# Second batch's scores moved ahead of its exps and values, third batch's q loaded first, fourth batch's loads behind a gate

## The chip, the cores and the metric

One core of a Trainium2 chip runs one launch of the kernel. The metric is the device time of one execution in microseconds (us), as the median over runs. The core has TensorE (PE; its weight loads are listed as PEld), VectorE (DVE), ScalarE (ACT), GpSimd (POOL) and SyncE (SP, which here only issues DMAs).

## The reference

Attention with pooled keys and values, then a mixer of two parts. With B = 8 batches, H = 8 heads, S = 576 positions and D = 64:

```
k_p = k.reshape(B, H, S/8, 8, D).mean(axis=3)          # 72 pooled keys; v_p likewise
attn = softmax(q @ k_p.T / sqrt(D)); a = attn @ v_p
x = a as (B, S, 512)
u = x + (relu(x.T @ w_tok1) @ w_tok2).T                # mix over positions, hidden 256
out = u + relu(u @ w_ch1) @ w_ch2                      # mix over channels, hidden 1536
```

All inputs and the output are float32; the kernel works in bfloat16 and casts as it loads.

## The kernel before

Batches are counted from 0. The 576 positions of a batch are 512 "main" rows (four tiles of 128) and 64 "tail" rows. Batches are paired, [0,7], [1,2], [3,4], [5,6], so that two tails share one tile of 128 rows; a pair's first batch has slot 0, the other slot 1. For batches 3 to 6 the tails of a pair's k and q are loaded with its first batch.

*Loads.* All go through GpSimd's DMA queue. `load(b, which)` (L116) issues k (0), q (1) and v (2) in the order given. k and q have two buffers each, v one. From batch 2 on, v comes as 72 rows of 8 positions (L131), and `sum_v` (L292) pools it on GpSimd with 12 additions (L298 to L300). `load_gated` (L737) first copies one column of a tile on GpSimd, so that the loads behind it are issued only when that tile is written, then loads, then pools v. GpSimd does all this in program order: an addition that waits for v holds up the next gate and the next loads.

*Attention.* A `Unit` (L302) holds two of the four main tiles of a batch; a batch has units `a` and `c`, and a `TailUnit` `t`. Their steps: q transposed (qT); scores `do_S` in three banks, each with a maximum and a subtraction on DVE (L329, L331); exps `do_E` on ACT (L339); the probabilities transposed, `do_PT` (pT); values `do_AV` (L387), each half followed by a reciprocal and a product on DVE (L391, L392). For batches 0 and 1 TensorE makes the transposes and DVE or ACT copies them out of PSUM (L352). From batch 2 on, SP issues DMA transposes: `qT_dma` (L538), pT (L346, L445).

*Mix over positions.* `mix_stream` (L567) adds `do_AT` (L472), k pooled for batches that come (`pool_k`: L267 on TensorE, L280 on DVE and ACT), then u (L510) and its transposes uT (L526, by SP's DMA from batch 1 on, one for each of the four tiles).

*Mix over channels.* `c_stream(b)` (L797): GT (L756, 12 tiles of 128 hidden channels), then the output (L771), added to u on DVE (L775) and stored by SP (L803). This is most of TensorE's work.

*Order.* Streams are lists of steps with costs. `weave` (L29) lays the attention and position mix of the next batches between the matmuls of the current batch's channel mix, in proportion to the costs; the order within each engine is then fixed. Beside batch 0's channel mix stand `second_stream` (batch 1's attention and mix, L645) and `score_stream(2)` (L689); beside batch 1's stand `value_stream(2)` (L718) and `score_stream(3)`. `value_stream(2)` begins with `qT_dma(3)` and with `load_gated(4, ...)`, whose gate is batch 2's last pT; its mix pools batch 3's k. `score_stream(3)` pools batch 4's k between its score banks.

Before the manual schedule, the kernel queues batch 1's loads, the last weights, batch 2's loads, batch 3's k and q, and `sum_v(2)`. Batch 3's v follows in `second_stream`, with `sum_v(3)` behind it.

Of the kernel before, what the change touches and what calls it, by code (L numbers as in the profile page):

```python
# [15 lines left out]
class Stream:  # L16
# [5 lines left out]
    def add(self, cost, fn):  # L22
        self.items.append((cost, fn))
# [25 lines left out]
def kernel(  # L49
# [20 lines left out]
    MAIN = NJ * P  # L70
# [37 lines left out]
    x_main, x_tail, u_main, uT_main, u_tail, uT_tail, ATs = {}, {}, {}, {}, {}, {}, {}  # L108
# [7 lines left out]
    def load(b, which=(0, 1, 2)):  # L116
        g = group_of[b]
        if (b == 2 or g > 1 and slot_of[b] == 0) and 0 in which:
            tail_t[b] = [tail_pool.tile([P, H, D], BF16, name=n) for n in ("kt", "qt")]
            if b == 2:  # L120
                for t in tail_t[b]:
                    nc.gpsimd.memset(t[half[0]], 0.0)
            else:
                tail_t[groups[g][1]] = tail_t[b]
        main_t.setdefault(b, [None] * 3)
        for i in which:
            src = (k, q, v)[i]
            if i == 2 and b > 1:

                vs = v_pool.tile([P, H, POOL, D], BF16, name="vs")  # L130
                nc.gpsimd.dma_start(out=vs[0:SP].rearrange("p h t d -> p h (t d)"),  # L131
                                    in_=src[b].rearrange("h (p t) d -> p h (t d)", t=POOL))
                main_t[b][i] = vs
                continue
            mt = (v_pool.tile([P, H, POOL, D], BF16, name="vs")[:, :, 0:NJ, :] if i == 2 else
                  kv_pool.tile([P, H, NJ, D], BF16, name=("km", "qm")[i]))
            main_t[b][i], tt = mt, tail_t[b][i]
            nc.gpsimd.dma_start(out=mt.rearrange("p h j d -> p h (j d)"),
                                in_=src[b, :, 0:MAIN, :].rearrange("h (p j) d -> p h (j d)", j=NJ))

            for bb in [b] if g < 2 else groups[g] if slot_of[b] == 0 else []:
                nc.gpsimd.dma_start(out=tt[half[slot_of[bb]]], in_=src[bb, :, MAIN:S, :].rearrange("h p d -> p h d"))
# [101 lines left out]
    def load_w_ch2():  # L244
        for i in range(3):
            n = NM // 3
            nc.gpsimd.dma_start(out=wc2[:, i * n:(i + 1) * n, :],
                                in_=moe_w_ch2[i * n * P:(i + 1) * n * P, :].rearrange("(c p) n -> p c n", p=P))
# [43 lines left out]
    def sum_v(b):  # L292

        vs, add = main_t[b][2][0:SP], ALU.add
        for h0 in range(0, H, 2):
            hs = slice(h0, h0 + 2)
            s4 = sum_pool.tile([P, 2, 4, D], FP32, name="s4")[0:SP]
            nc.gpsimd.tensor_tensor(out=s4, in0=vs[:, hs, 0:4], in1=vs[:, hs, 4:8], op=add)  # L298
            nc.gpsimd.tensor_tensor(out=s4[:, :, 0:2], in0=s4[:, :, 0:2], in1=s4[:, :, 2:4], op=add)  # L299
            nc.gpsimd.tensor_tensor(out=vpx[b % NB][:, hs, 0:D], in0=s4[:, :, 0], in1=s4[:, :, 1], op=add)  # L300

    class Unit:  # L302
# [40 lines left out]
        def do_PT(self, e):  # L343
            self.pT[e] = pt_pool.tile([P, H, P], BF16, name="pT")
            if not self.by_pe:
                nc.sync.dma_start_transpose(out=self.pT[e], in_=self.probs[:, e].rearrange("p h n -> p (h n)"))  # L346
                return
            pT_ps = ps_tr.tile([SP, H, P], BF16, name="pt")
            for h in range(H):
                nc.tensor.transpose(out=pT_ps[:, h, :], in_=self.probs[:, e, h, 0:SP], identity=ident)  # L350
            by_dve = e == 0 and self.jj == 1 if self.first else e == 1
            (nc.vector.tensor_copy if by_dve else nc.scalar.copy)(out=self.pT[e][0:SP], in_=pT_ps)  # L352

        def do_AV(self, e):
# [189 lines left out]
    KP, VP, QT, SC, PT, AV = 900, 1080, 900, 1060, 700, 1150  # L544
    parts = {}

    def units(b):

        g, s = group_of[b], slot_of[b]
        x_main[b] = x_pool.tile([P, NJ, DM], BF16, name="xm")  # L550
        t = None
        if g < 2:
            t = TailUnit(g, [b])
        elif s == 0:
            x_tail[g] = x_pool.tile([P, DM], BF16, name="xt")
            t = TailUnit(g, groups[g])
        parts[b] = Unit(b, 0), Unit(b, 1), t
        qTs[b] = att_pool.tile([P, 2 * H, P], BF16, name="qT")
        return parts[b]
# [4 lines left out]
    def adder(st):  # L564
        return lambda weight, f, *args, **kw: st.add(weight, lambda: f(*args, **kw))

    def mix_stream(st, b, pooled=()):  # L567

        g, s = group_of[b], slot_of[b]
        add = adder(st)  # L570
        u_main[b] = u_pool.tile([P, NJ, DM], BF16, name="um")
        uT_main[b] = u_pool.tile([P, 4, MAIN], BF16, name="uTm")
        if s == 1:
            u_tail[g] = ut_pool.tile([P, DM], BF16, name="ut")
            uT_tail[g] = ut_pool.tile([P, 4, P], BF16, name="uTt")
        do_AT, do_both_AT, do_u, do_uT = token_mix(b)
        if b == 0:
            return do_both_AT, do_u, do_uT
        add(1080, do_AT, 0)
        add(1080, do_AT, 1)  # L580
        for bb in pooled:
            add(KP, pool_k, bb)
        nj = NJ + s
        for j in range(nj + 1):
            if j < nj:
                add(690, do_u, j)
            if j >= 1:
                add(0 if b else 224, do_uT, j - 1)
# [56 lines left out]
    def second_stream(st):  # L645

        add = adder(st)
        b = 1
        a, c, t = units(b)
        add(QT, a.do_qT)  # L650
        add(QT, c.do_qT)
        add(SC, a.do_S, 0)
        add(VP, pool_v, b)
        add(SC, a.do_S, 1)
        add(0, a.do_E, 0)
        add(SC, a.do_S, 2)
        add(0, a.do_E, 1)
        add(SC, c.do_S, 0)
        add(0, a.do_E, 2)
        add(QT, t.do_qT)  # L660
        add(SC, c.do_S, 1)
        add(0, c.do_E, 0)
        add(PT, a.do_PT, 0)
        add(PT, a.do_PT, 1)
        add(SC, t.do_S)
        add(0, c.do_E, 1)
        add(AV, a.do_AV, 0)
        add(SC, c.do_S, 2)
        add(0, t.do_E)
        add(0, load, 3, (2,))  # L670
        add(0, sum_v, 3)
        add(AV, a.do_AV, 1)
        add(0, c.do_E, 2)
        add(PT, t.do_PT)
        add(PT, c.do_PT, 0)
        add(AV, t.do_AV)
        add(PT, c.do_PT, 1)
        units(2)
        add(0, qT_dma, 2)
        add(AV, c.do_AV, 0)  # L680
        add(AV, c.do_AV, 1)
        mix_stream(st, b, owned(2))

    def owned(b):

        g, s = group_of[b], slot_of[b]
        return [b] if g < 2 else groups[g] if s == 0 else []
# [134 lines left out]
    clear_probs()  # L822
    load(1)
    load_w_ch2()
    load(2)
    load(3, (0, 1))
    sum_v(2)
    engines = {mybir.EngineType.PE, mybir.EngineType.Activation, mybir.EngineType.DVE,
               mybir.EngineType.SP, mybir.EngineType.Pool}
    with tc.manual_schedule(engines=engines):  # L830
        weave(Stream(), first_stream())
        for b in range(B):
            side = Stream()
            if b == 0:
                second_stream(side)
            elif b + 1 < B:
                value_stream(side, b + 1)
            if b + 2 < B:
                score_stream(side, b + 2)

            weave(c_stream(b), side, 3456.0 if b <= 1 else 1728.0, 3456.0 if b == B - 2 else 1728.0)
# [30 lines left out]
```

## Time and profile before

| | us |
|---|---|
| median of 3 runs | 289.02 |
| lowest and highest | 288.86, 290.66 |
| the profiled execution | 290.2 |
| its span | 288.5 |
| TensorE busy in the span | 271.0 (94%) |
| VectorE busy | 162.4 (56%) |
| ScalarE busy | 121.3 (42%) |
| GpSimd busy | 101.5 (35%) |

The span runs from the first to the last instruction of one profiled execution; 1.7 us lie around it. A line of the profile names an engine, a line of the kernel, an operation, the tile that it writes and those that it reads (`out<-in`), and how many such instructions stand together. "<-" in brackets names what ended the idle time before. The granted clock is the share of TensorE's full clock. GpSimd's and SP's DMAs are two queues that share 16 DMA engines.

### The profile page before, as it was taken

Reading aid. Unit: us, or ns where it says so; the run is one execution under the profiler, and the core shown is the slowest. Engines: PE = TensorE matmul, PEld = TensorE weight load, DVE = VectorE, ACT = ScalarE, POOL = GpSimd, SP = SyncE. Lnnn points to the kernel's source line nnn. Section 1 sums busy time; section 2 is a strip of 40 time slices with the busy share of each in tenths; the row PEclk is TensorE's granted clock in tenths of the full one; section 3 lists DMA queues with packets and bytes.
Section 4 is the critical chain, followed back from the end, with each engine's and each line's share of the span. In section 5 each row is a group of like instructions: output and inputs, shape, how many; then the busy total and the mean of one; then the engine's idle time right before and its main releaser. Section 6 shows DMA issues by size and latency. Waiting matters only on the chain.

```text
span 288.5 us, 5632 instructions
## 1 busy us (share of the span) xinstructions
PE 271.0 (94%) x2210; PEld 147.1 (51%) x2246; DVE 162.4 (56%) x371; ACT 121.3 (42%) x222; POOL 101.5 (35%) x147
## 2 busy tenths in 40 slices
PE   6888998885999999999999999999999999999995
PEld 4554755442445554446545554465445444464463
DVE  4676268687356985386647953684558642530012
ACT  8572887113442355114553365035442561026320
POOL 8666634292780836129508423570000000000000
PEclk9999999999899999999999999999999999999999
DMA  7999999999959999998999799959524820241013
GB/s 84 185 205 198 196 204 192 174 203 146 252 88 169 166 214 195 182 183 166 172 185 155 170 218 153 157 165 162 115 54 97 194 58 36 93 109 39 27 45 110
DMA packets 102714, 42.68 MB, mean 148 GB/s; under 512 B 72480, under 2 KB 98080, under 8 KB 102688
## 3 DMA queue, kind: packets, MB, share of 16 engines
q0 software_dynamic: 36688, 17.93, 47.2%
q1 hardware_dynamic: 65856, 24.26, 43.7%
q8 instruction: 17, 0.28, 0.4%
q10 hardware_dynamic: 144, 0.13, 0.1%
q14 instruction: 9, 0.07, 0.1%
HBM read 35.85 MB, written 9.44 MB: 157 GB/s over the span
## 4 chain that ended last, share of the span: by engine, by line
PE 82%; DMA 7%; DVE 6%; ACT 3%; issue 1%; DVEq 0%
PE pa L756 31%; PE pa L771 28%; DMA qT<-qm 4%; PE pa L510 4%; PE pa L472 4%; PE pa L387 3%; DMA uTm<-um 3%; PE pa L253 2%; PE pa L326 2%; DVE sh L331 2%; DVE mx L329 1%; PE pa L267 1%; ACT prob_m L339 1%; PE pa L518 1%; ACT pT L352 1%
## 5 line engine op out<-in xcount | busy, mean ns | idle before, releaser
L771 PE MATMUL pa<-wc,GT 128*128 128x512 bf16 (+1 forms) x429 | 102.7, 373 | 1.0 <-DVE sh L331 0.2
L756 PE MATMUL pa<-uTm,wc 128*128 128x512 bf16 x357 | 90.1, 384 | 3.8 <-DMA uTm<-um 3.1
L758 ACT ACTIVATE GT<-pa 128x512 bf16<-128x512 f32 x105 | 62.5, 597 | 66.5 <-PE pa L756 62.4
L756 PEld LDWEIGHTS <-wc 128*128 128x128 bf16 x564 | 45.4, 98 | 40.6 <-DVE o L775 3.6
L771 PEld LDWEIGHTS <-GT 128*128 128x128 bf16 x444 | 41.5, 98 | 40.4
L339 ACT ACTIVATE prob_m<-sh 128x432 bf16<-128x432 f32 (+1 forms) x48 | 24.7, 522 | 60.9 <-DVE sh L331 51.1
L298 POOL TENSOR_TENSOR s<-vs 72x512 f32<-72x512 bf16 x24 | 27.6, 1148 | 49.7 <-DMA vs<-in_v_dram 48.2
L775 DVE TENSOR_TENSOR o<-pa,um 128x512 f32<-128x512 f32 (+1 forms) x33 | 22.1, 670 | 25.3 <-PE pa L771 25.3
L329 DVE TENSOR_REDUCE mx<-pa 128x6 f32<-128x432 f32 (+1 forms) x48 | 26.4, 550 | 7.6 <-PE pa L326 7.5
L331 DVE TENSOR_TENSOR sh<-pa,mx 128x432 f32<-128x432 f32 (+1 forms) x48 | 26.8, 558 | 5.1 <-DVE mx L329 0.5
L391 DVE RECIPROCAL den<-pa 128x4 f32<-128x4 f32 (+1 forms) x66 | 11.6, 176 | 24.5 <-PE pa L387 24.4
L515 DVE TENSOR_TENSOR um<-pa,xm 128x512 bf16<-128x512 f32 x30 | 20.2, 687 | 8.6 <-PE pa L510 8.6
L392 DVE TENSOR_TENSOR xm<-pa,den 128x256 bf16<-128x256 f32 x56 | 23.8, 424 | 1.9
L510 PE MATMUL pa<-AT,w2m 128*128 128x512 bf16 x64 | 18.3, 379 | 0.5 <-ACT AT L466 0.5
L299 POOL TENSOR_TENSOR s<-s 72x256 f32<-72x256 f32 x24 | 17.3, 722 | 1.9
L468 DVE TENSOR_SCALAR AT<-pa 128x512 bf16<-128x512 f32 x8 | 5.5, 692 | 21.8 <-PE pa L476 21.1
L387 PEld LDWEIGHTS <-pT 72*128 72x128 bf16 (+1 forms) x280 | 12.4, 100 | 8.8 <-issue 1.7
L326 PE MATMUL pa<-kbd,qT 128*128 128x144 bf16 x128 | 15.5, 226 | 1.4 <-DMA qT<-qm 0.9
L326 PEld LDWEIGHTS <-qT 128*128 128x128 bf16 x128 | 10.7, 98 | 10.5 <-DMA qT<-qm 1.4
L387 PE MATMUL pa<-vpx,pT 72*128 72x65 bf16 (+1 forms) x280 | 14.1, 194 | 1.1 <-DVE pT L352 0.5
L472 PE MATMUL pa<-xm,w1m 128*128 128x512 bf16 x54 | 14.4, 379 | 0.4 <-DVE xm L392 0.2
L253 PE MATMUL pa<-idle 128*128 128x288 bf16 (+2 forms) x40 | 9.8, 379 | 2.3 <-DVE pool_t L178 2.2
(122 smaller groups left out, 232.8 us busy)
## 6 DMA issues: line engine op xcount, KB each, us to landing
out_dram<-o SPq DMA_DIRECT2D x31, 256.0 KB, 2.6
km<-in_k_dram POOLq DMA_DIRECT2D x8, 512.0 KB, 7.7
qm<-in_q_dram POOLq DMA_DIRECT2D x7, 512.0 KB, 12.7
vs<-in_v_dram POOLq DMA_DIRECT2D x6, 576.0 KB, 10.1
wc<-in_moe_w_ch_dram POOLq DMA_DIRECT2D x6, 512.0 KB, 12.4
out_dram<-o SPq DMA_DIRECT2D x9, 128.0 KB, 2.4
vs<-in_v_dram POOLq DMA_DIRECT2D x2, 512.0 KB, 9.9
kt<-in_k_dram POOLq DMA_DIRECT2D x8, 64.0 KB, 7.7
```

What stands on the lines that cost most here:

```text
L298: nc.gpsimd.tensor_tensor(out=s4, in0=vs[:, hs, 0:4], in1=vs[:, hs, 4:8], op=add)
L326: nc.tensor.matmul(out=sc[:, (h - h0) * 2:(h - h0) * 2 + 2, :], lhsT=qTs[self.b][:, 2 * h + self.jj, :], rhs=kbd[self.b % NB][:, h], start ...
L329: nc.vector.tensor_reduce(out=mx[:, 0:n], in_=sc, axis=AX.X, op=ALU.max)
L331: nc.vector.tensor_tensor(out=sh[:, 0:n], in0=sc, in1=mx[:, 0:n, None].broadcast_to([P, n, SP]), op=ALU.subtract)
L339: nc.scalar.activation(out=self.probs[:, :, h0:h1, 0:SP].rearrange("p e h n -> p h e n"), in_=self.sh[i][:, 0:(h1 - h0) * 2].rearrange("p ...
L387: nc.tensor.matmul(out=ao[r, hh, :], lhsT=probs_of(h, r), rhs=vpx[b % NB][:, h, :], start=True, stop=True)
L392: nc.vector.tensor_tensor(out=xo[rows, hf * HP * D:(hf + 1) * HP * D].rearrange("p (h d) -> p h d", d=D), in0=ao[rows, :, 0:D], in1=den[ro ...
L472: nc.tensor.matmul(out=at_ps, lhsT=w1m[:, j, m * P:(m + 1) * P], rhs=x_main[b][:, j, :], start=(j == 0), stop=False)
L510: nc.tensor.matmul(out=u_ps, lhsT=w2m[:, m, j, :], rhs=ATs[b][:, m, :], start=(m == 0 and not by_act), stop=(m == 1))
L756: nc.tensor.matmul(out=g_ps[:, i, :], lhsT=wc1[:, kk, m * P:(m + 1) * P], rhs=uTs[:, kk, :], start=(kk == 0), stop=(kk == 3))
L758: nc.scalar.activation(out=GT[:, m0:m0 + per, :], in_=g_ps, func=AF.Relu)
L771: nc.tensor.matmul(out=hold["ps"], lhsT=GT[:, kk, j * P:(j + 1) * P], rhs=wc2[:, kk, cols], start=(kk == 0), stop=(kk == NM - 1))
```

## The change

In `second_stream`, batch 2's v and `sum_v(2)` are queued behind batch 1's pooled v. The transposes and value products of unit `a` move back behind the tail's scores and the third score bank of unit `c`. `a`'s second value product stands behind the tail's transpose, and both transposes of `c` stand together ahead of the tail's value product. c's second pT copy goes from DVE to ACT. Ahead of the schedule, batch 2's loads are q, then k; batch 3's k and q are no longer queued there. All of batch 3's loads, v too, and `sum_v(3)` stand at the end of `second_stream` behind a gate on the last main tile of batch 1's transposed u.

```
-            by_dve = e == 0 and self.jj == 1 if self.first else e == 1
+            by_dve = e == 0 and self.jj == 1 if self.first else e == 1 and self.jj == 0
...
         add(VP, pool_v, b)
+        add(0, load, 2, (2,))
+        add(0, sum_v, 2)
         add(SC, a.do_S, 1)
...
         add(PT, a.do_PT, 0)
-        add(PT, a.do_PT, 1)
         add(SC, t.do_S)
         add(0, c.do_E, 1)
-        add(AV, a.do_AV, 0)
+        add(PT, a.do_PT, 1)
         add(SC, c.do_S, 2)
         add(0, t.do_E)
-        add(0, load, 3, (2,))
-        add(0, sum_v, 3)
-        add(AV, a.do_AV, 1)
+        add(AV, a.do_AV, 0)
         add(0, c.do_E, 2)
         add(PT, t.do_PT)
+        add(AV, a.do_AV, 1)
         add(PT, c.do_PT, 0)
+        add(PT, c.do_PT, 1)
         add(AV, t.do_AV)
-        add(PT, c.do_PT, 1)
         units(2)
         add(0, qT_dma, 2)
         add(AV, c.do_AV, 0)
         add(AV, c.do_AV, 1)
         mix_stream(st, b, owned(2))
+        add(0, load_gated, 3, lambda: uT_main[b][:, 3, MAIN - 1:MAIN])
...
-    load(2)
-    load(3, (0, 1))
-    sum_v(2)
+    load(2, (1, 0))
```

In the built program the order of TensorE's, DVE's and ACT's instructions differs only inside this stretch, and SP's not at all. GpSimd now works through: batch 2's q, k and v, `sum_v(2)`, the gate, batch 3's seven loads, `sum_v(3)`, the gate of batch 4, batch 4's loads.

## The prediction

> Batches are counted from 0, as in the code: the "second batch" is batch 1, the "third" batch 2, the "fourth" batch 3. Times without a unit are us from the start of the span.
>
> **What bounds the kernel now.** I read the page first (busy shares and the row of the granted clock), then the stretches of 5 us, the chain of waits from 40 to 100, and the timelines of GpSimd and TensorE. TensorE is busy 94% of the span, so only its gaps can be won, and a new gap costs its full length.
>
> ```profile
> PE 271.0 (94%) x2210; PEld 147.1 (51%) x2246; DVE 162.4 (56%) x371; ACT 121.3 (42%) x222; POOL 101.5 (35%) x147
> ```
> The stretches show where the gaps lie: behind "PE" stands its busy time, and the third value from the end is the granted clock.
> ```profile
> 65.00:70.00 5.00, 3.30 (x21) 1.58 (x19) 4.53 (x10) 2.11 (x5) 1.39 (x3) 1.00 1.49 144
> 70.00:75.00 5.00, 3.51 (x9) 1.30 (x10) 1.01 (x2) 1.13 (x3) 1.78 (x2) 0.66 1.15 213
> 75.00:80.00 5.00, 4.95 (x44) 2.58 (x43) 2.88 (x11) 2.98 (x5) 4.53 (x7) 1.00 1.14 251
> ```
> The chain names the causes: the transpose of batch 2's q (qT) is issued at 49.10 and takes 12.50, and the last transpose of batch 1's u (uTm) takes 7.32 from 64.03 to 71.35. Then 16 matmuls take 5.24.
> ```profile
> 49.10 12.50 DMA qT<-qm
> ...
> 64.03 7.32 DMA uTm<-um
> 71.35 0.14 issue
> 71.49 5.24 PE pa L756 x16
> ```
> GpSimd's timeline decides what the change costs. GpSimd works in order: loads, the 12 additions of sum_v, a gate copy, the next batch's loads. The idle time before an instruction stands in brackets.
> ```profile
> 65.06 0.86 POOL L131 DMA_DIRECT2D vs<-in_v_dram  x1
> ...
> 73.14 1.15 POOL L298 TENSOR_TENSOR s<-vs 72x512 f32<-72x512 bf16 x1 [6.73 <-DMA vs<-in_v_dram]
> ...
> 83.24 0.19 POOL L739 COPY gate<-pT 128x1 bf16<-128x1 bf16 x1
> 83.36 0.92 POOL L138 DMA_DIRECT2D km<-in_k_dram  x1
> ...
> 110.31 0.19 POOL L739 COPY gate<-pT 128x1 bf16<-128x1 bf16 x1 [6.16 <-DMA pT<-prob_m]
> ...
> 127.74 1.15 POOL L298 TENSOR_TENSOR s<-vs 72x512 f32<-72x512 bf16 x1 [11.58 <-DMA vs<-in_v_dram]
> ```
> Batch 3's v (issued 65.06) releases sum_v(3) at 73.14, and 10.1 later batch 4's k is issued (83.36). TensorE pools that k here:
> ```profile
> 94.51 0.69 PE L267 MATMUL pa<-pool_m,km 128*64 128x64 bf16 x32
> ```
>
> **Gains.** *Loads.* Batch 3's k, q and four tails (2 x 512 + 4 x 64 = 1280 KB) leave the stretch before 64. From 46 to 53 GpSimd's queue moved 1.35 MB in 7 us, 193 KB/us, so 6.6 us of queue time go. Batch 2's q takes k's place: k landed by 46.2 (the issue that waits for it is at 46.24) and q by 49.1, so q lands some 2.9 earlier, and qT starts at 46.2. Batch 2's v then lands at 52.4 (49.45 + 576/193) to 55.5 (as now). k, now 2.9 later at 49, is first used at 56.4: nothing. Its qT had to share with loads until 64; now they end by 55, and qT lands at 55 to 57. TensorE's wait of 0.94 for it (at 61.65) goes.
>
> *Second stream.* TensorE's short waits from 43 to 54 are 0.39 (pT copy), 0.76 (prob_t), 0.52 (DVE's pT copy) and 0.25 (xm): 1.9. Scores of the tail and of c's third bank now stand ahead of the value products, so the first two go. The pT copy of c moves from DVE (0.68) to ACT (0.99) and makes two such copies stand in line there, so I leave 0.5 of the waits. Gain 1.4; bounds 0 and 1.9. The same matmuls run in both.
>
> *uT.* The last uTm issue is at 64.03, now 62.6. That line's transposes take from issue to landing 2.4 least, 3.3 median, 7.8 most; with no load beside them I take 3.1, so it lands at 65.7. TensorE, which finished its work at 68.36, comes 2.3 earlier, at 66.0. So 3.13 of waiting goes, and the clock's loss with it: 16 matmuls at 0.216 are 3.46, they took 5.24, 1.78 lost. In all 1.4 + 0.94 + 3.13 + 1.78 = 7.3 by the time the first value product of batch 2 stands (76.57, now 69.3).
>
> **Costs.** *Gate.* The gate copy waits for that uTm (65.7) and for sum_v(2), which ends 10 after batch 2's v: 62.5 to 65.5. So batch 3's loads start at 65.7: 6 issues moved past sum_v(2) (0.9 + 1.4 + 0.9 + 1.4 = 4.6 us of GpSimd) and v behind them, issued at about 71 instead of 65.06. SP's queue keeps its order.
>
> *v(3).* Nobody but GpSimd waits for it, but behind it stand sum_v(3), gate(4) and batch 4's k. The same seven loads in the same order stand behind the gate at 110.31, whose v was in place at 127.74: 17.4. Lower bound: 1856 KB at 193 KB/us are 9.6, and 2.4 to the first packets, 12. Upper: from 57 to 62, with transposes in the other queue, GpSimd's queue moved 0.43 MB in 5 us, 86 KB/us; 21.6 + 2.1 = 23.7. I take 17.4, the row nearest in kind.
>
> *Sum.* 65.7 + 17.4 = 83.1; sum_v(3) 10.1 (73.14 to 83.24) ends at 93.2; gate 0.1; k(4) takes 6.2 (the one issued at 83.36) to 7.8 (140.61), I take 6.8: **100.1**. TensorE needs it at 94.51 less 7.3. It works in order, so everything behind waits, and pooling begins 100.1 - 94.5 = 5.6 later than before. The clock: after the 3.13 us of idle time it stood at 0.50 and cost 1.78; after 0.94 of idle time it stayed at 1.00. The wait is some 6 to 10 us, so I take 1.8 (bounds 0 and 1.8). Total 5.6 + 1.8 = **+7.4**.
>
> *Under cover.* The value products of batch 2 will stall too: their last pT is issued 1.75 earlier (DVE's chain of scores is what moves least), at 73.3, and lands 3.3 (alone) to 7.8 (beside loads) later, at 76.6 to 81.1; TensorE asks for it at 81.1 - 7.3 = 73.8. These 3 to 7 us are hidden by the wait for k(4), 13 us long from 87.2; without that cover they alone would take most of the gain. q(3), issued near 68, lands near 77 (8.9 by the median of its line), its transpose by 86 to 90 (12.5 beside loads), needed at 94: nothing. sum_v(4) had 6.16 spare before the gate at 110.31 and comes some 10 later beside work 7 later: 3 left.
>
> From 100 on TensorE is the bound, and nothing gives the loss back. The profiled execution took 290.2 (span 288.5), 1.2 above the median 289.0. From 290.2 the sum is 297.6; from the median **296.4**, which I predict.
>
> **A rule beside a row.** From 68 to 72, with v(3) in flight, GpSimd's queue moved 0.52 MB and SP's 0.09 MB: the loads crowd the transposes out. The Trainium skill (DMA: Bandwidth & Descriptors, "Queues, rings and completion order") says that an engine takes turns between the queues that have work, packet by packet. This row disagrees (0.52 against 0.09 MB), the stretch from 57 to 62 agrees (0.43 against 0.37 MB). Were turns the rule throughout, the fourth rival below would hold, near 302.7.
>
> **Rivals.**
> 1. *The forecast*: v(3) late, so k(4) late. 293 to 300.5.
> 2. *Faster*: the loads of batch 3 stay hidden and 7.3 remains: 281.7. It needs k(4) by 87.2, hence v(3) by 70.2, 4.5 after the gate; over 1% faster needs k(4) by 89.8, v(3) 7.1 after the gate. For it: v alone took 7.9 from its issue. Against: 1280 KB now stand before it, and the rows have 17.4.
> 3. *Loads at full rate*: 12 from gate to v gives k(4) at 94.7, +0.2 and the clock 1.8: 291.0. For: 187 to 199 KB/us from 114 to 118. Against: pT of batch 2 (640 KB), two outputs (512) and qT of batch 3 (640) fall in this stretch.
> 4. *Equal shares*: 23.7, 6.3 more than forecast: 302.7. For: 57 to 62. Against: the row of 17.4 and 68 to 72.
> 5. *The change doesn't do what it says*: uTm stays at 71.35, nothing is won, the gate opens 5.7 later: 302. For: outputs still share SP's queue. Against: the load that ran beside uTm is v(3), and it is gone from there.
>
> **How the numbers follow.** Chances: forecast 0.66, faster 0.04, full rate 0.12, equal shares 0.12, no earlier uTm 0.06. The range 290.5 to 301.5 holds the forecast and the full rate and leaves out the rest, part of which falls short of it: about 0.2. About 1% (2.9 us) is what a measurement of this kernel can tell from no change: below 286.1 only the second rival, 0.04; within, most of the third, 0.10; above 291.9 the rest, 0.86.
>
> **What would show it.** Right: no wait for uTm near 66 and clock 1.00 there; qT landing by 57; the gate near 66; sum_v(3) starting near 83; gate(4) near 93; a wait of TensorE of several us for km before the second L267 group near 100, the clock near 0.5 behind it. Wrong: sum_v(3) starting by 72 (rival 2) or 78 (3), or pooled k without a wait. The weakest term is the 17.4.

## The result, and the profile after

The changed kernel takes 305.13 us (median of 4 runs, 304.38 to 306.83) and the kernel before, run beside it, 289.84 (288.86 to 291.94): a ratio of 1.053 with a 95% interval of 1.045 to 1.061. It is slower, as forecast, but by 15.3 us instead of 7.4, and it lies above the range. The profiled execution took 304.38 with a span of 302.7, which is 14.2 more than the span before.

The page of the changed kernel. TensorE's busy time grew by 6.9: a halved clock makes the same matmuls longer, and the trace of the kernel before has 36 matmul records fewer, which may be part of it. The row PEclk, the granted clock in 40 slices of 7.6 us, has a dip of two slices from 76 to 91 and one of a slice behind 106:
```profile
PE 277.9 (92%) x2246; PEld 148.0 (49%) x2246; DVE 162.1 (54%) x370; ACT 121.6 (40%) x223; POOL 101.7 (34%) x148
...
PEclk9999999998559969999999999999999999999999
```
The stretches of 5 us put times to it. The third value from the end is the granted clock; the two behind it are the DMA engines' share and GB/s:
```profile
65.00:70.00 5.00, 4.93 (x30) 2.15 (x28) 4.08 (x11) 3.02 (x7) 4.60 (x7) 1.00 0.96 142
70.00:75.00 5.00, 1.79 (x13) 0.56 (x12) 1.52 (x5) 1.26 (x4) 0.93 (x2) 0.89 1.45 168
75.00:80.00 5.00, 2.47 (x12) 0.94 (x12) 1.14 (x4) 0.51 (x2) 0.00 (x0) 0.50 1.47 171
80.00:85.00 5.00, 2.33 (x12) 0.87 (x12) 1.12 (x4) 1.00 (x2) 0.00 (x0) 0.50 1.44 167
85.00:90.00 5.00, 3.14 (x15) 1.48 (x16) 1.12 (x4) 0.60 (x1) 0.44 (x1) 0.50 1.21 160
...
100.00:105.00 5.00, 2.13 (x15) 1.03 (x12) 3.63 (x6) 0.56 (x1) 2.42 (x3) 0.96 0.84 102
105.00:110.00 5.00, 2.95 (x45) 1.83 (x46) 0.92 (x2) 1.35 (x3) 0.00 (x0) 0.50 1.25 191
```
Before, 65 to 70 (3.30 busy) and 70 to 75 (3.51 busy, clock 0.66) were bad. That dip is won: from 65 to 70 TensorE is now busy for 4.93 of 5 us at full clock. In its place stand six bad stretches.

The chain of waits of the changed kernel names what carries the end (start, duration, work):
```profile
62.83 2.46 DMA uTm<-um
...
65.34 0.19 POOL gate L740
...
70.07 19.35 DMA vs<-in_v_dram
89.56 1.14 POOL s L298
...
99.77 7.24 DMA km<-in_k_dram
...
107.05 1.07 PE pa L267 x32
```
The last transpose of batch 1's u, which took 7.32 before, takes 2.46. The gate opens at 65.34. Batch 3's v is issued at 70.07 and takes 19.35; ten microseconds of sum_v(3) follow, then batch 4's k, and at 107.05 TensorE pools that k, as against 94.51 before. These 12.54 and some 1.7 of lost clock behind them are the 14.2 of the span.

TensorE's timeline of the changed kernel shows all of its waits (in brackets) between 65 and 110:
```profile
65.43 3.62 PE L757 MATMUL pa<-uTm,wc 128*128 128x512 bf16 x16
...
73.06 0.43 PE L387 MATMUL pa<-vpx,pT 72*128 72x65 bf16 x8 [2.90 <-DMA pT<-prob_m]
...
77.31 0.65 PE L387 MATMUL pa<-vpx,pT 72*64 72x65 bf16 x8 [2.62 <-DMA pT<-prob_t]
...
80.93 0.62 PE L387 MATMUL pa<-vpx,pT 72*128 72x65 bf16 x8 [1.16 <-DMA pT<-prob_m]
...
86.86 0.62 PE L387 MATMUL pa<-vpx,pT 72*128 72x65 bf16 x8 [3.60 <-DMA pT<-prob_m]
...
107.05 1.07 PE L267 MATMUL pa<-pool_m,km 128*64 128x64 bf16 x32 [4.92 <-DMA km<-in_k_dram]
```
The 16 matmuls at 65.43 have no wait and take 3.62 instead of 5.24. The first of the five value products of batch 2 runs at 68.88 without a wait. Before it stood here:
```profile
76.57 0.42 PE L387 MATMUL pa<-vpx,pT 72*128 72x65 bf16 x8
```
That is 7.7 earlier: the gain did come. It is spent at the other four, which wait 10.3 in all for their transposed probabilities (pT), with the clock at 0.50 from 75 to 90; the last of them runs at 86.86 instead of 81.29. When TensorE pools batch 3's k (93.95, before 86.39), it is 7.6 late. The wait of 4.92 for batch 4's k comes on top.

Where the time of v(3) went is told by the DMA queues (packets, MB, share of the 16 engines' time; the shares can add up to more than 100%, because packets overlap in time; q0 is GpSimd's, q1 SP's). In the changed kernel from 68 to 89:
```profile
q0 software_dynamic: 4974, 1.90, 80.8%
q1 hardware_dynamic: 4177, 1.49, 57.4%
```
This is 161 KB/us in all. For the row from which the forecast took 17.4 (batch 5's loads before, 112.7 to 127.7) it is 170 KB/us in all:
```profile
q0 software_dynamic: 4976, 1.90, 104.2%
q1 hardware_dynamic: 1271, 0.65, 30.6%
```
The total rate is nearly the same; there is more than twice as much in SP's queue. Two shorter windows of the changed kernel show how the queues share. First, from 76 to 82:
```profile
q0 software_dynamic: 1810, 0.56, 85.3%
q1 hardware_dynamic: 1789, 0.45, 61.4%
```
There are as many packets of the one as of the other. That is what turns packet by packet would give, as the Trainium skill states them (DMA: Bandwidth & Descriptors, "Queues, rings and completion order"), if the profile's packets are the packets of that rule. The prediction, which let the row of 68 to 72 speak against it, leaned the wrong way; it also compared megabytes, where the rule counts packets. In packets that row is 520 to 356. Now from 69 to 72, at the start of the loads:
```profile
q0 software_dynamic: 882, 0.42, 120.4%
q1 hardware_dynamic: 28, 0.00, 1.6%
```
Here SP's queue got next to nothing, though a pT transpose issued at 65.55 was in flight until 73.02. So equal turns agree with the middle of the burst and not with its start.

### The profile page after: what moved, and what is told of

It reads as the page before. It is cut to its first block, busy times and chain, and to the rows that moved or that the text cites. A ratio compares the mean times of both kernels' runs of the same rounds, so it can differ in the third digit from the quotient of the medians.

```text
span 302.7 us, 5669 instructions
## 1 busy us (share of the span) xinstructions
PE 277.9 (92%) x2246; PEld 148.0 (49%) x2246; DVE 162.1 (54%) x370; ACT 121.6 (40%) x223; POOL 101.7 (34%) x148
## 4 chain that ended last, share of the span: by engine, by line
PE 74%; DMA 11%; POOL 6%; DVE 5%; ACT 2%; issue 1%; DVEq 0%; POOLq 0%
PE pa L772 28%; PE pa L757 27%; DMA vs<-in_v_dram 6%; PE pa L510 4%; PE pa L472 3%; PE pa L387 2%; DMA km<-in_k_dram 2%; PE pa L326 2%; DMA qm<-in_q_dram 2%; POOL s L298 2%; PE pa L267 1%; DVE sh L331 1%; DVE um L515 1%; DVE mx L329 1%; POOL s L299 1%
## 5 line engine op out<-in xcount | busy, mean ns | idle before, releaser
L772 PE MATMUL pa<-wc,GT 128*128 128x512 bf16 (+1 forms) x444 | 105.7, 378 | 0.0
L757 PE MATMUL pa<-uTm,wc 128*128 128x512 bf16 x372 | 92.8, 388 | 0.1
L339 ACT ACTIVATE prob_m<-sh 128x432 bf16<-128x432 f32 (+1 forms) x48 | 24.6, 522 | 60.5 <-DVE sh L331 50.7
L387 PE MATMUL pa<-vpx,pT 72*128 72x65 bf16 (+1 forms) x280 | 14.7, 199 | 10.3 <-DMA pT<-prob_m 7.7
L472 PE MATMUL pa<-xm,w1m 128*128 128x512 bf16 x56 | 15.4, 398 | 0.3 <-DVE xm L392 0.3
```

The lines of the kernel that those rows point to most:

```text
L339: nc.scalar.activation(out=self.probs[:, :, h0:h1, 0:SP].rearrange("p e h n -> p h e n"), in_=self.sh[i][:, 0:(h1 - h0) * 2].rearrange("p ...
L387: nc.tensor.matmul(out=ao[r, hh, :], lhsT=probs_of(h, r), rhs=vpx[b % NB][:, h, :], start=True, stop=True)
L472: nc.tensor.matmul(out=at_ps, lhsT=w1m[:, j, m * P:(m + 1) * P], rhs=x_main[b][:, j, :], start=(j == 0), stop=False)
L757: nc.tensor.matmul(out=g_ps[:, i, :], lhsT=wc1[:, kk, m * P:(m + 1) * P], rhs=uTs[:, kk, :], start=(kk == 0), stop=(kk == 3))
L772: nc.tensor.matmul(out=hold["ps"], lhsT=GT[:, kk, j * P:(j + 1) * P], rhs=wc2[:, kk, cols], start=(kk == 0), stop=(kk == NM - 1))
```

## The experiments

My theory after the result: the loss is the path gate, v(3), sum_v(3), k(4); v(3) is late because the pT transposes, outputs and qT(3) in SP's queue take their turns beside the burst; the same meeting makes pT late and gives TensorE four covered waits. The rivals: the new order of batch 1's steps costs something itself; the gate (the issue time), not the sharing, sets the loss; moving k(4) forward is enough to have the gain. Each ratio below is against the kernel before on the same chip. Its median was 291.08 in the first four experiments, 291.01 in the next four and 290.39 in the last three; the recorded ratios differ by up to 0.5% from the quotient of the medians. In the diffs, "+" and "-" are against the changed kernel unless it says otherwise.

### k(4) ahead of sum_v(3)
```
     def load_gated(b, ready):
         nc.gpsimd.tensor_copy(out=gate, in_=ready())
-        load(b, (0, 2, 1) if slot_of[b] else (0, 1, 2))
+        load(b, (2, 1) if b == 4 else (0, 2, 1) if slot_of[b] else (0, 1, 2))
+        if b == 3:
+            load(4, (0,))
         sum_v(b)
```


> The change with one issue moved: batch 4's k is loaded right behind batch 3's v, ahead of sum_v(3), instead of behind it; everything else as changed. Theory A (two costs, one over the other): the gated loads make batch 2's pT late (last value product at 86.9 where before had 81.3) and, through v(3) and sum_v(3), k(4) late (107.05 against 94.51); the second covers the first. Then the wait for k(4) goes, the value products still wait some 10 us in all, and pooling of k(4) comes 13.2 behind the last value product plus 1.7 of half clock, near 101.8: about +7.3 on the time before, 296 to 298. Theory K (k(4) alone costs): back to 290 or below. Theory P (the value products alone cost): 303 or more.

Measured: 301.89, ratio 1.034 (1.027 to 1.040), span 299.5: between the theories, far from the 296 to 298 of the first. k(4) was pooled at 99.56 without a wait, so that path is cut; but it was still 5.05 later than before, because the waits at batch 2's value products stayed (3.11, 2.37, 1.22, 1.77), as the prediction's "under cover" step says. I had not foreseen what came next on TensorE's timeline:
```profile
114.62 0.43 PE L387 MATMUL pa<-vpx,pT 72*128 72x65 bf16 x8 [4.22 <-DMA pT<-prob_m]
```
Batch 4's v and q, issued behind sum_v(3) at 99.5 to 101.3, now met batch 3's first pT, issued at 104.66 and landed at 114.57. 5.05, 4.22 and 1.7 of clock (0.66 from 115 to 120) make the 11.0 of the span. Of the change's 14.2 only 3.2 went with the chain through k(4): the waits at the value products use up the gain and leave TensorE 5 late by themselves, and a new collision took most of the rest.

### The new order of steps alone
The kernel before with only the new order of `second_stream` and the pT copy on ACT; its loads stay:
```
-            by_dve = e == 0 and self.jj == 1 if self.first else e == 1
+            by_dve = e == 0 and self.jj == 1 if self.first else e == 1 and self.jj == 0
...
         add(PT, a.do_PT, 0)
-        add(PT, a.do_PT, 1)
         add(SC, t.do_S)
         add(0, c.do_E, 1)
-        add(AV, a.do_AV, 0)
+        add(PT, a.do_PT, 1)
         add(SC, c.do_S, 2)
...
```


> The kernel before with the new order of batch 1's steps alone (and the pT copy of c on ACT); all loads, and their order, as before. Theory A: the order itself is worth what was forecast, 1.4 us by the products of batch 1 (first L472 group at about 51.4), and costs nothing elsewhere; q(2)'s transpose still lands near 61.6, so TensorE waits some 2.3 there; whether the last transpose of batch 1's u, now issued 1.4 earlier, gets past v(3)'s load decides between 285 and 290. A rival (the second copy on ACT and the later copies of a make batch 1's products late): 291 or more.

Measured: 290.53, ratio 0.998 (0.995 to 1.002): no difference. The steps come earlier, and the group behind batch 1's uT starts at 69.36 after a wait of 1.24, with the clock at 1.00 (71.49 and 3.13 before). But the gain is given back where other data do not come earlier: TensorE's timeline has a wait of 2.55 for qT(2) at 61.41 (0.94 before), 2.29 at 75.26 for a pT, and 0.77 and 1.01 further on.

### The new loads alone
The changed kernel with the old order of steps and the pT copy on DVE:
```
-            by_dve = e == 0 and self.jj == 1 if self.first else e == 1 and self.jj == 0
+            by_dve = e == 0 and self.jj == 1 if self.first else e == 1
...
         add(PT, a.do_PT, 0)
+        add(PT, a.do_PT, 1)
         add(SC, t.do_S)
         add(0, c.do_E, 1)
-        add(PT, a.do_PT, 1)
+        add(AV, a.do_AV, 0)
         add(SC, c.do_S, 2)
...
```


> The change's loads and gate alone, with the order of batch 1's steps and the DVE copy as before. Theory A: the gate opens 1.0 to 1.5 later (66.5 to 67), the value products of batch 2 and k(4) wait as in the change, so all of the loss is here: 304 to 307. A rival (the new order of steps carries part of the loss): below 303.

Measured: 307.8, ratio 1.053 (1.043 to 1.062), a little above the 304 to 307 of the theory. The whole loss is in the loads; the first rival falls. The gate opens at 67.76 and v(3) is in place 24.6 later (24.2 in the changed kernel): the number holds with the order of the steps exchanged.

### Batch 3's loads without the gate
```
         add(0, load, 2, (2,))
+        add(0, load, 3, (0, 1))
         add(0, sum_v, 2)
...
         mix_stream(st, b, owned(2))
-        add(0, load_gated, 3, lambda: uT_main[b][:, 3, MAIN - 1:MAIN])
+        add(0, load, 3, (2,))
+        add(0, sum_v, 3)
```


> The change without its gate: batch 2 is loaded q, k, v, and batch 3's k and q stand right behind it in GpSimd's queue; v(3) and sum_v(3) follow sum_v(2). Theory A: q(2) still lands near 45.5 and its transpose by 59; k(4) is issued near 83 as before and is no wait; v(3) falls on batch 2's first pT, which costs up to 3 us and a half clock behind it: 283 to 288. A rival (the early q and k, not the gate, make the loss): 295 or more.

Measured: 291.97, ratio 1.002 (0.999 to 1.005). The loss is gone with the gate (k(4) pooled at 96.06 without a wait), and the gain does not come either, against my 283 to 288. Its timeline of TensorE has the old collision again:
```profile
61.01 0.36 PE L326 MATMUL pa<-kbd,qT 128*128 128x144 bf16 x3 [1.71 <-DMA qT<-qm]
...
71.95 6.33 PE L759 MATMUL pa<-uTm,wc 128*128 128x512 bf16 x16 [4.24 <-DMA uTm<-um]
```
In both places batch 3's 1.9 MB meet some of SP's transposes: qT(2) and uT(1) here, pT(2) behind the gate.

### v(3) first among the gated loads
```
-        load(b, (0, 2, 1) if slot_of[b] else (0, 1, 2))
+        load(b, (2, 0, 1) if b == 3 else (0, 2, 1) if slot_of[b] else (0, 1, 2))
```


> The change with batch 3's loads behind the gate in the order v, k, q instead of k, q, v. The chain in question runs from v(3) over sum_v(3) to k(4). Theory A: v(3) is there 9 to 10 after the gate (near 75) instead of 24, sum_v(3) ends near 85.5, k(4) is issued there as in the kernel before and TensorE does not wait for it, nor, since batch 4's loads end by 101, for batch 3's pT. The value products of batch 2 wait as in the change, which left 5.0 at k(3) and k(4) in the run with k(4) ahead: +5 to +6, 295 to 297. A rival (q(3), now last, delays its transpose past batch 3's first scores): 299 or more.

Measured: 303.97, ratio 1.040 (1.031 to 1.048), against the 295 to 297 of the theory. v(3) was in place 10.3 after the gate (65.35 to 75.65) and k(4) was issued at 85.84, 14 earlier than in the changed kernel, with no wait for k. The time hardly moved, because of the rival named in the expectation:
```profile
105.54 0.54 PE L326 MATMUL pa<-kbd,qT 128*128 128x144 bf16 x3 [6.83 <-DMA qT<-qm]
```
q(3) is last now and takes 18.2 from its issue at 68.70. Only then is its transpose issued, at 86.89, and it falls on batch 4's loads (issued from 85.84 to 88.5): 18.6 from issue to landing.

### Batch 2's probabilities transposed by TensorE
The same work in another place: unit and tail of batch 2 make pT as batches 0 and 1 do, on TensorE with copies by ACT and DVE, so that 640 KB leave SP's queue. `do_PT` of batch 2 moves from `score_stream(2)` into `value_stream(2)`, and the gate of batch 4 copies 72 rows instead of 128:
```
-            self.b, self.jj, self.first, self.by_pe = b, jj, b == 0, b <= 1
+            self.b, self.jj, self.first, self.by_pe = b, jj, b == 0, b <= 2
...
-            self.g, self.bs, self.first, self.by_pe = g, bs, 0 in bs, min(bs) <= 1
+            self.g, self.bs, self.first, self.by_pe = g, bs, 0 in bs, min(bs) <= 2
...
+        if b == 2:
+            add(PT, a.do_PT, 0)
+            add(PT, a.do_PT, 1)
+            add(PT, t.do_PT)
+            add(AV, a.do_AV, 0)
+            add(PT, c.do_PT, 0)
+            add(AV, a.do_AV, 1)
+            add(PT, c.do_PT, 1)
             add(0, load_gated, b + 2, lambda: c.pT[1][:, 0, 0:1])
```


> The change with batch 2's pT made on TensorE (36 transposes and 5 copies more) instead of by SP's DMA: 640 KB in packets of 256 bytes less beside batch 3's loads. Theory A (the two queues take turns packet by packet, so the small packets of the transposes hold the loads up): no wait at batch 2's value products, the transposes cost TensorE 2.1, and v(3) is there 18 to 20 after the gate instead of 24.2; k(4) is then pooled near 102, so 299 to 301. A rival (the loads are slow by themselves: HBM, or GpSimd's issue): still 24 from the gate, 304 or more.

Measured: 297.09, ratio 1.017 (1.010 to 1.024), span 295.5. No value product waits. GpSimd's timeline, at the first addition of sum_v(3), and TensorE's, at the pooling of k(4):
```profile
82.39 1.14 POOL L298 TENSOR_TENSOR s<-vs 72x512 f32<-72x512 bf16 x1 [11.44 <-DMA vs<-in_v_dram]
```
```profile
99.38 1.06 PE L267 MATMUL pa<-pool_m,km 128*64 128x64 bf16 x32 [8.96 <-DMA km<-in_k_dram]
```
The gate opened at 65.36, so v(3) took 17.0: the 17.4 of the forecast, once the pT are out of the other queue, and less than the 18 to 20 expected. The queues from 68 to 82, 165 KB/us in all:
```profile
q0 software_dynamic: 4920, 1.87, 113.6%
q1 hardware_dynamic: 779, 0.42, 26.0%
```
The changed kernel moved 1.07 MB more in SP's queue in its window; at 165 that is 6.5 us, and v(3) came 7.2 later. This decides between sharing and the gate: same gate, same loads, other company. k(4) is pooled 4.9 later than before, and with the clock behind a wait of 8.96 the last matmuls come 6.3 later; the other 0.7 of the span's +7.0 lie behind them. It is about the size that I had forecast for the change, by the path that I had forecast.

### Both: pT on TensorE and v(3) first
Against the kernel of the section before:
```
-        load(b, (0, 2, 1) if slot_of[b] else (0, 1, 2))
+        load(b, (2, 0, 1) if b == 3 else (0, 2, 1) if slot_of[b] else (0, 1, 2))
```


> Both: batch 2's pT on TensorE and batch 3's v first behind the gate. Theory A: both costs of the change are gone, and its gain shows, 7.3 less 2.1 for the transposes on TensorE: about 5 under the kernel before, 284 to 287. A rival (there is a third cost, or the gain is given back at a later wait): 290 or more.

Measured: 292.70, ratio 1.005 (1.001 to 1.008); 284 to 287 was expected. k(4) is pooled at 91.01, 3.5 earlier than before, and then it is given back:
```profile
102.06 3.54 PE L771 MATMUL pa<-uTm,wc 128*128 128x512 bf16 x8 [3.12 <-DMA uTm<-um]
```
Batch 4's loads, issued at 84.5 to 87, now meet batch 2's uT.

### Only v(3) behind the gate
The new order of steps with the old loads, except that v(3) alone waits for batch 1's uT, and k(4) and q(4) stand ahead of sum_v(3) behind batch 2's last pT:
```
+    def load_v3():
+        nc.gpsimd.tensor_copy(out=gate, in_=uT_main[1][:, 3, MAIN - 1:MAIN])
+        load(3, (2,))
...
+        if b == 4:
+            load(4, (0, 1))
+            sum_v(3)
+            load(4, (2,))
```


> A version meant to beat both: the kernel before with the new order of batch 1's steps, its early loads kept, but only batch 3's v behind the gate on batch 1's last transposed u, and batch 4's k and q issued at batch 2's last pT ahead of sum_v(3), batch 4's v behind it. Theory A: the last transpose of u no longer shares with v(3), so the wait at the first L756 group falls below 1.3 with the clock at 1.00; batch 2's first pT is before v(3); k(4) is there before 88; the wait of 2.3 for q(2)'s transpose stays: 284 to 287. A rival (v(3), later, falls on batch 2's last three pT): 289 to 292.

Measured: 293.27, ratio 1.009 (1.004 to 1.013): a little above the rival's 289 to 292, far from 284 to 287. v(3), 576 KB issued at 69.39, falls on batch 2's pT (2.98 of wait at 78.08 for the tail's), and qT(2) keeps a wait of 1.95. The wait behind uT is 1.18, as against 1.24 with the new order alone: holding v(3) back saved next to nothing there. The last uT, issued at 62.74, took 6.4 although v(3) was not yet issued; packets of batch 3's earlier loads ran beside it until 66, and what slowed it from 66 to 69, with SP's queue alone at work, is open.

### k(4), then k(4) and q(4), ahead of sum_v(3), with pT on TensorE
Against the kernel with batch 2's pT on TensorE; the second one has `(2,)` for `(2, 1)` and `load(4, (0, 1))`:
```
-        load(b, (0, 2, 1) if slot_of[b] else (0, 1, 2))
+        load(b, (0, 1, 2) if b == 3 else (2, 1) if b == 4 else (0, 2, 1) if slot_of[b] else (0, 1, 2))
+        if b == 3:
+            load(4, (0,))
         sum_v(b)
```


> Batch 2's pT on TensorE, gate as in the change, loads of batch 3 in its order (k, q, v), and batch 4's k right behind v(3), ahead of sum_v(3); batch 4's v and q follow at its gate, near 92.5. Theory A (TensorE waits wherever a transpose by SP's DMA falls into a batch's loads): no wait at batch 2's value products, none for k(4), and batch 2's transposed u (86 to 95) has the DMA engines to itself; what is left is batch 3's first pT (near 96 to 100) beside v(4) and q(4), a wait of 1 to 4: 286 to 291. A rival (the gain of the gate is not there at all): 292 or more.

> As the one before, with batch 4's q also ahead of sum_v(3), so that only v(4) (576 KB) stands behind it. Theory A: v(4) is over by 98, batch 3's first pT is nearly alone, and no wait over 1 us is left behind 60; q(4) now shares with batch 3's qT, which lands near 89, just ahead of batch 3's first scores: 285 to 288. A rival (qT of batch 3 comes late and takes the place of the wait): 290 or more.

Measured: 295.34, ratio 1.018 (1.015 to 1.022), and 294.64, 1.015 (1.012 to 1.019); both expectations are missed by some 4 to 7 us. The profiled execution of the first, 297.39, is the slowest of its six and lies some 3 us behind the other versions with pT on TensorE from 55 on. In the first, k(4) comes without a wait, but batch 4's v and q (from 95.3 on) hold batch 3's pT from 98.35 to 109.69:
```profile
109.74 0.62 PE L387 MATMUL pa<-vpx,pT 72*128 72x65 bf16 x8 [6.66 <-DMA pT<-prob_m]
```
In the second, v(4) is all that is left there, and TensorE waits for the pooled v (vpx) of batch 4 instead. The tail's value products are those of batches 3 and 4 together, and sum_v(4) runs only from 100.03 to 110.1: v(4) is issued behind sum_v(3), at 92.08, and sum_v(3) starts late (81.86) because v(3) stands behind batch 3's k and q. GpSimd's first addition of sum_v(4), and TensorE's two waits:
```profile
100.03 1.14 POOL L298 TENSOR_TENSOR s<-vs 72x512 f32<-72x512 bf16 x1 [7.08 <-DMA vs<-in_v_dram]
```
```profile
107.67 0.25 PE L387 MATMUL pa<-vpx,pT 72*64 72x65 bf16 x4 [1.10 <-POOL vpx L300]
...
110.22 0.23 PE L387 MATMUL pa<-vpx,pT 72*64 72x65 bf16 x3 [2.30 <-POOL vpx L300]
```

### All three: pT on TensorE, v(3) first, k(4) and q(4) ahead of sum_v(3)
Against the kernel with batch 2's pT on TensorE:
```
-        load(b, (0, 2, 1) if slot_of[b] else (0, 1, 2))
+        load(b, (2, 0, 1) if b == 3 else (2,) if b == 4 else (0, 2, 1) if slot_of[b] else (0, 1, 2))
+        if b == 3:
+            load(4, (0, 1))
         sum_v(b)
```


> As the one before, with batch 3's loads in the order v, k, q, then batch 4's k and q. Theory A: sum_v(3) ends near 84.5 and v(4) is loaded from there to 91; q(3) is 4 later, so batch 3's qT stands beside k(4), q(4) and v(4) from 82 to 91 and lands near 91, one or two us late; batch 2's transposed u shares the start of that: 287 to 290. A rival (the order does not matter once k(4) and q(4) are ahead): equal to the one before within 0.5%.

Measured: 288.88, ratio 0.995 (0.992 to 0.998), span 286.2: the one version clear of noise below the kernel before, by 0.5%. Two of TensorE's waits for a DMA or a late step are left between 85 and 106:
```profile
90.56 0.36 PE L326 MATMUL pa<-kbd,qT 128*128 128x144 bf16 x3 [1.28 <-DMA qT<-qm]
...
102.38 1.90 PE L773 MATMUL pa<-uTm,wc 128*128 128x512 bf16 x8 [0.55 <-DVE sh L331]
```
sum_v(3) starts at 75.02 here and sum_v(4) at 94.27, and the tail's products at 106.20 have no wait. k(4) is pooled at 91.90, 2.6 earlier than before. Of the 7.7 that the early part wins, 2.0 go to the transposes that TensorE now makes itself (four groups that hold up the next matmul by 0.45 each and one by 0.22), 1.28 to the wait for qT(3), 0.48 to one on DVE at 79.87 and 0.55 to the one at 102.38, which leaves 3.4. The last matmuls come 3.0 earlier than before (274.00 against 277.05) and the span is 2.3 shorter; the rest I have not traced.

## Why the prediction was wrong

*Early order, qT(2), uT.* Right. The last matmul of batch 1's first mix group came 1.9 earlier (1.4 forecast, bounds 0 to 1.9); qT(2) landed at 56.0 (55 to 57) and its wait is gone; uT landed at 65.29 (65.7), no wait, clock 1.00. Won by the first value product: 7.7 (7.3). The reason given for uT, that v(3) is the load beside it, is only part of it: with v(3) alone held back, the last uT still took 6.4, and only with all of batch 3's loads behind the gate 2.46.

*Gate.* 65.34 against 65.7. Right.

*v(3).* This step failed: 17.4 was taken, 24.2 was measured, 0.5 above the upper bound of 23.7 (which adds 2.1 to the first packets where the lower bound adds 2.4; with 2.4 it is 24.0). The row was the nearest in kind of load and not in company. It had 0.65 MB of SP's beside it. The prediction itself lists, against its third rival, what would stand beside v(3): pT, outputs and qT of batch 3, 1.79 MB. It used them to exclude the low end and did not price them. With the row's total of 170 KB/us, 1.86 and 1.79 MB take 21.5, and with the 2.4 to the first packets 23.9. Rival 4, equal shares, came nearest to what happened, at a chance of 0.12, although the start of the burst was not shared: it stood for +13.7, and the spans differ by 14.2. With batch 2's pT out of SP's queue, the same step measured 17.0.

*sum_v(3), gate(4), k(4).* 10.1 and 7.24 (10.1 and 6.8 forecast). Right. k(4) is pooled at 107.05 instead of 100.1, and of these 7.0 the v term is 6.8.

*Clock.* 1.7 against 1.8. Right.

*Under cover.* The place was right and the size was not: 10.3 of waits and some 5.0 of lost clock, 15.3 in all by the pooling of batch 3's k, instead of 3 to 7. That is twice the gain of 7.7. I had priced the last pT alone; four of the five meet the burst. In this kernel the loss is covered by k(4), as forecast; with k(4) ahead of sum_v(3) it showed as the 5 us that stay when the cover goes.

*Range.* It left out rival 4. A term of which the text says that it is the weakest, with an upper bound worth 302.7, should have had that bound in the range.

## What to carry to other kernels

A load's duration is not a property of the load: as a first estimate, take all bytes that both queues will move in its stretch, and divide by the total rate that the trace shows for such company (here 161 to 170 KB/us in the three bursts above; with loads alone it was 195 from 46 to 53 and 181 from 114 to 118 before), before taking a row of the same load with other company. In these runs a burst that was moved out of the way of one latency-critical transpose landed on another; list what SP issues in the new place, and who waits for it, before counting the gain. And in an in-order queue a load is not needed by its reader alone, but by all that stands behind its reader: the value products that read v(3) stood at 105.18 before, while k(4), queued behind sum_v(3), was wanted at 87.2 (94.51 less the 7.3 to be won).

## What was unexpected of the hardware

The two queues moved as many packets each in the middle of a burst (1810 and 1789 from 76 to 82), but at its start the loads went nearly alone for some 3 us (882 and 28 from 69 to 72); why is open, and no run here took that apart. The last uT took 2.46 with no load beside it, 7.32 in the kernel before, and 6.4 with only v(3) held back; qT took 12.5 beside batch 3's loads before, and 18.6 beside batch 4's when v(3) was first. And waits of 2.90, 2.62, 1.16 and 3.60 with a few us of work between them kept the granted clock at 0.50 from 75 to 90, although the first of them alone is shorter than the 3.13 that halved it for some 3 us before. Behind the 2.90 the clock was still 1.00 from 73 to 73.5 and 0.50 from 74 on. Single waits of 2.55 and 2.29 with the new order alone left it at 1.00; a wait of 2.98 with only v(3) held back was followed by 0.50.
